# Tokens 512 to 1023 of a mixture unit as one block of 512, and the attention steps in another order

## The chip, the cores and the metric

The kernel runs on one core of one Trainium2 chip. The metric is the device time of one execution, in microseconds (us), as the median of several runs. The core has five engines with a queue each: TensorE (PE; its weight loads are listed as PEld), VectorE (DVE), ScalarE (ACT), GpSimd (POOL) and SyncE (SP, which here only issues DMAs).

## The reference, cut to what matters

```python
# 1. attention with a decaying state: B=2 batches, H=8 heads, S=768 tokens, D=48
for t in range(S):
    cur = einsum('bhd,bhe->bhde', u[None] * k[t], v[t])
    y[:, :, t] = einsum('bhd,bhde->bhe', r[t], state + cur)
    state = w[None, :, :, None] * state + einsum('bhd,bhe->bhde', k[t], v[t])
x = y.transpose(0, 2, 1, 3).reshape(1536, 384)
# 2. mixture of 4 units, all of them dense: w1[e] is 384x1024, w2[e] is 1024x384
p = probs / (probs.sum(-1) + 1e-9)
for e in range(4):
    out += p[:, e:e+1] * (relu(x @ w1[e]) @ w2[e])
# 3. one more layer pair with ELU, 384 -> 2048 -> 384
g = where(h > 0, h, exp(min(h, 0)) - 1), h = out @ w_in
return g @ w_out
```

## The kernel before, in words

Every product of the layers is computed in three matmuls, since each operand is split into a high and a low part: high times high, low times high, high times low. For weights the parts are wh and wl, for x they are xh and xl, for the hidden values hh and hl. Features lie on the partitions and tokens on the free axis.

**Units and rows.** `layers` (L877) runs over six units `u` (four of the mixture, two halves of the last pair), over blocks of tokens that start at `t0` and have `n` tokens, and over eight slices `f` of 128 hidden features. One turn of the inner loop is called a row here. A row has one group of nine matmuls into a bank `ph` (`st1`, L721, matmuls at L732), then the evacuation of ph (`evac`, L739): hh on ScalarE (L744) and hl on VectorE (L745). Two rows later follows the second product, nine matmuls into `po` (`st2`, L760, matmuls at L770); that of a block's last slice comes ahead of the row's evacuation. After a block `evac1` (L779) multiplies po by the probabilities `pb` on VectorE (L788). Two banks `ph` take turns. In the first unit, tokens 0 to 1023 are four blocks of 256 and tokens 1024 to 1535 one block of 512; in all later units every block has 512.

**Weights.** `load` and `load_next` (L541) fetch slices of 128x768 from SP's queue. `split` (L573) makes wh on ScalarE (L580) and wl on VectorE (L581). In the first unit `work` makes one such split at the end of each row until its eight slices are done. While `paced` is set, a load waits until the third load ahead of it has landed. Three raw slices have a buffer.

**Attention.** It runs in twelve chunks of 128 tokens, six for each batch, and shares the engines with the rows of the first unit. Chunks 0 and 1 come before the first row. The steps of a chunk c are:

- scaling, `s1h` (L231): r and k, transposed (rkT), by tables of powers of w, two multiplies on VectorE;
- u times k times r, `s1u` (L248, L250, tile uk), and the keys for the state, `s1k` (L241, tile kp): on POOL, from rk;
- the sum of uk over each head, `s1d` (L256), on VectorE; then the diagonal of the scores' tile A: `s1g` (L261) on POOL, `s1e` (L267) on ScalarE;
- scores, `s2` (L298), into two banks of `pa`;
- mask, `s2p` (L305): VectorE copies the scores of earlier keys from those banks into A, whose diagonal holds the sums and whose other half holds zeros;
- output, `s3` (L356): the state's part (L368), the next chunk's scores if `more` is set, the state's new part `s3u` (L320, in a ph bank), and A times v (L377); then VectorE makes the new state S (`s3s`, L341), ScalarE copies the result (yT, L384), and for every second chunk the transposed result goes through DRAM (xd, xs; L389, L393);
- state scaling, `s3w` (L353), on ScalarE, which the next `s3s` needs;
- `s4`: xh on ScalarE and xl on VectorE or POOL of 256 tokens (L534, L535).

**Order.** The order of instructions on each engine is that of the program. `fast` (L923) builds a list `steps`; `before` hands each row some of them: after the row's ph group and ahead of its evacuation (early) or behind the evacuation (late). Four banks serve the attention in turn: scores take the first two, outputs the last two (`at.own`, `bank`).

## Time and profile before

| what | value |
|---|---|
| median of 3 runs | 648.69 us (648.41 to 648.79) |
| the profiled execution | 648.31 us, its span 646.5 us |
| PE busy | 638.5 us, 99% of the span |
| PEld, DVE, ACT, POOL busy | 83%, 50%, 35%, 33% |
| granted TensorE clock, mean of the span | 0.998 |
| matmuls of 512 columns at L732, high times high | 384, 389 ns each |
| the same with 256 columns | 96, 290 ns each |

Times in the profile count from the span's first instruction. The duration of one matmul overlaps that of the next, so the pace is read from a whole group of nine and not from one matmul. An idle time is shown in square brackets ahead of the row that ended it, with what released it. The first row of the first unit begins at 16.0 us, the block of tokens 1024 to 1535 at 117.6 us.

### The profile page before, as it was taken

To read this page: it belongs to the slowest core of one execution; us is meant where nothing else is said; L and a number is where in the kernel's file an instruction comes from. 1 tells how busy PE (TensorE), PEld (TensorE's weight loads), DVE (VectorE), ACT (ScalarE), POOL (GpSimd) and SP (SyncE) were. 2 spreads that over 40 slices of the span, in tenths; PEclk is the share of its full clock that TensorE was granted. 3 is DMA by queue.
4 is the path that set the end of the run, shared out by engine and by line. 5 is a ranking of instruction groups with operands and counts; after the bars stand their busy time and mean duration, and the time that the engine had idled before them with its cause. 6 is when DMAs were issued, how large, how long until landed. Compare 5 with 4: busy or idle time off the path is not lost.

```text
span 646.5 us, 9506 instructions
## 1 busy us (share of the span) xinstructions
PE 638.5 (99%) x3843; PEld 536.9 (83%) x3845; DVE 324.8 (50%) x461; ACT 226.3 (35%) x414; POOL 210.6 (33%) x179
## 2 busy tenths in 40 slices
PE   8999999999999999999999999999999999999997
PEld 6799999888888888888888888888888888888885
DVE  7776654445545455554545456566667653112122
ACT  7732333332211131211132112123646464544441
POOL 7854672100031212130312132342754434333331
PEclk9999999999999999999999999999999999999999
DMA  8884563334131143411216231318441342001011
GB/s 243 272 289 119 153 176 114 112 99 147 49 98 30 68 154 115 167 54 50 97 58 242 99 115 50 97 34 314 190 148 37 110 146 98 1 0 50 1 50 54
DMA packets 27593, 72.72 MB, mean 112 GB/s; under 512 B 3266, under 2 KB 8436, under 8 KB 27540
## 3 DMA queue, kind: packets, MB, share of 16 engines
q1 hardware_dynamic: 22640, 59.41, 28.4%
q10 hardware_dynamic: 4900, 12.61, 5.1%
q8 instruction: 32, 0.52, 0.3%
q14 instruction: 21, 0.17, 0.1%
HBM read 55.08 MB, written 16.93 MB: 111 GB/s over the span
## 4 chain that ended last, share of the span: by engine, by line
PE 92%; DMA 5%; DVE 1%; POOL 1%; issue 1%; SPq 0%; ACT 0%; DVEq 0%
PE ph L732 44%; PE po L770 44%; DMA raw<-in_ws_dram 3%; DMA pb<-pd 1%; DMA rk<-in_rkv_dram 1%; PE po L914 1%; PE pa L298 1%; PE pa L377 1%; PE pa L368 1%; PE po L377 0%; PE ph L320 0%; SPq L543 0%; POOL uk L250 0%; POOL uk L248 0%; DVE hl L745 0%
## 5 line engine op out<-in xcount | busy, mean ns | idle before, releaser
L732 PE MATMUL ph<-xh,wh 128*128 128x512 f32 (+1 forms) x480 | 174.5, 369 | 0.4 <-DVE hl L745 0.3
L770 PE MATMUL po<-hh,wh 128*128 128x512 f32 (+1 forms) x471 | 173.9, 369 | 0.0
L732 PE MATMUL ph<-xh,wl 128*128 128x512 f32 (+1 forms) x480 | 173.8, 368 | 0.0
L770 PE MATMUL po<-hl,wh 128*128 128x512 f32 (+1 forms) x471 | 173.0, 367 | 0.0
L770 PE MATMUL po<-hh,wl 128*128 128x512 f32 (+1 forms) x471 | 173.0, 367 | 0.0
L744 ACT ACTIVATE hh<-ph 128x512 fp32r<-128x512 f32 (+1 forms) x112 | 60.0, 536 | 260.6 <-PE ph L732 260.4
L745 DVE SCALAR_TENSOR_TENSOR hl<-ph,hh 128x512 fp32r<-128x512 f32 (+1 forms) x112 | 68.4, 612 | 158.1 <-ACT hh L744 157.8
L732 PE MATMUL ph<-xl,wh 128*128 128x512 f32 (+1 forms) x480 | 124.7, 368 | 0.0
L732 PEld LDWEIGHTS ph<-xh,wh 128*128 128x128 f32 x480 | 90.4, 188 | 16.2 <-DVE hl L745 0.5
L732 PEld LDWEIGHTS ph<-xh,wl 128*128 128x128 f32 x480 | 90.5, 188 | 14.9
L770 PEld LDWEIGHTS po<-hh,wh 128*128 128x128 f32 x471 | 88.7, 188 | 16.3 <-issue 1.5
L757 POOL TENSOR_TENSOR hl<-g,hh 128x512 fp32r<-128x512 f32 x48 | 63.1, 1314 | 117.6 <-ACT hh L756 109.5
L770 PEld LDWEIGHTS po<-hl,wh 128*128 128x128 f32 x471 | 88.7, 188 | 14.7
L770 PEld LDWEIGHTS po<-hh,wl 128*128 128x128 f32 x471 | 88.7, 188 | 14.7
L732 PEld LDWEIGHTS ph<-xl,wh 128*128 128x128 f32 x480 | 85.9, 188 | 15.4 <-DVE xl L535 0.4
L643 POOL TENSOR_TENSOR nl<-a,wide 128x768 fp32r<-128x768 f32 x16 | 29.8, 1865 | 173.9 <-issue 106.1
L754 DVE SCALAR_TENSOR_TENSOR g<-m,ph 128x512 f32<-128x512 f32 x48 | 32.9, 686 | 104.6 <-ACT m L752 99.1
L792 POOL TENSOR_TENSOR acc<-acc,t 128x512 f32<-128x512 f32 x27 | 34.2, 1294 | 72.5 <-DVE t L791 72.5
L756 ACT CAST hh<-g 128x512 fp32r<-128x512 f32 x48 | 29.9, 622 | 43.0 <-DVE g L754 43.0
L751 ACT ACTIVATE m<-ph 128x512 f32<-128x512 f32 x48 | 28.7, 598 | 43.4 <-PE ph L732 36.7
L581 DVE TENSOR_TENSOR wl<-raw,wh 128x768 fp32r<-128x768 f32 x32 | 32.0, 1013 | 5.4 <-ACT wh L580 4.9
L752 ACT ACTIVATE m<-m 128x512 f32<-128x512 f32 x48 | 30.3, 632 | 1.5
(129 smaller groups left out, 487.2 us busy)
## 6 DMA issues: line engine op xcount, KB each, us to landing
raw<-in_ws_dram SPq DMA_DIRECT2D x32, 384.0 KB, 4.0
wide<-in_ws_dram SPq DMA_DIRECT2D x16, 768.0 KB, 5.1
w<-nh ACTq DMA_DIRECT2D x16, 384.0 KB, 2.4
w<-nl ACTq DMA_DIRECT2D x16, 384.0 KB, 5.7
wh<-w SPq DMA_DIRECT2D x16, 384.0 KB, 5.7
wl<-w SPq DMA_DIRECT2D x16, 384.0 KB, 6.6
rk<-in_rkv_dram SPq DMA_DIRECT2D x12, 384.0 KB, 5.8
rkT<-in_rkT_dram SPq DMA_DIRECT2D x10, 448.0 KB, 5.3
```

The source lines that it names most:

```text
L581: self.weng.tensor_tensor(out=lo, in0=t, in1=hi.bitcast(F32), op=ALU.subtract)
L643: nc.gpsimd.tensor_tensor(out=lo, in0=af, in1=cf, op=ALU.add)
L732: nc.tensor.matmul(ph[:, 0:n], a[:, kk, c0:c0 + P], b[:, kk], start=q == 0, stop=q == 3 * KD - 1)
L744: nc.scalar.activation(hh[:, 0:n], ph[:, 0:n], AF.Relu)
L745: nc.vector.scalar_tensor_tensor(out=hl[:, 0:n], in0=ph[:, 0:n], scalar=0.0, in1=hh[:, 0:n].bitcast(F32), op0=ALU.max, op1=ALU.subtract)
L751: nc.scalar.activation(m, ph, AF.Relu, scale=-1.0)
L752: nc.scalar.activation(m, m, AF.Exp, scale=-1.0)
L754: nc.vector.scalar_tensor_tensor(out=gg, in0=m, scalar=-1.0, in1=ph, op0=ALU.add, op1=ALU.max)
L756: nc.scalar.copy(hh, gg)
L757: nc.gpsimd.tensor_tensor(out=hl, in0=gg, in1=hh.bitcast(F32), op=ALU.subtract)
L770: nc.tensor.matmul(po, a[:, ff, i * P:(i + 1) * P], b[:, 0:n], start=f == 0 and q == 0 and not i * n % TB, stop=f == NF - 1 and q == 2 and ...
L792: nc.gpsimd.tensor_tensor(out=a, in0=a, in1=t[:, 0:n], op=ALU.add)
```

## The change

Tokens 512 to 1023 of the first unit become one block of 512, so the first unit has two blocks of 256 and two of 512. As this block needs x of all its tokens at its first row, the attention of chunks 0 to 7 now has to be over by the end of the second block; a table `plan` names for each block of the first unit (0, 1, 2), slice and place (E early, L late) what is done there. In it:

- the mask of a chunk stands behind the output of the chunk before it, and for chunks 3 and 4 behind rows of its own; the sum and the diagonal stand one row or more ahead of the mask. The second half of the diagonal is made on ScalarE for all chunks (`s1d`, `s1e`);
- chunk 4's scores are issued inside the output of chunk 3;
- for chunks 9 to 11, which run beside the block of 512, one result goes to a ph bank, and the state's new part comes behind A times v (`late`);
- the loads of chunks 3 and 4 stand earlier in SP's queue, between the raw slices; only the first unit's eight slices are loaded until `rest`, in the third block; pb is loaded in two pieces; after chunks 3 and 5 the next loads go ahead of the results' stores (`mid`);
- xl of s4 is made on VectorE, except after chunks 5 and 9;
- hh and hl have buffers of 512 tokens from the start; two tables of the start move to tiles that are written only later.

```diff
-NS = (3, 1, 1, 1, 1, 1, 1, 1)
...
+        self.prb = g.xp.tile([P, 2, NP, P], F32, tag="acc0", name="prb")
...
-        self.Tr = self.c.tile([P, NP, P], F32, name="Tr")
+        self.Tr = self.g.xp.tile([P, NP, P], F32, tag="acc1", name="Tr")
...
     def s1d(self, ci):
         self.a0[ci] = a0 = self.p2.tile([P, H], F32, tag="a0", name="a0")
         self.g.nc.vector.tensor_reduce(out=a0, in_=self.st[ci]["uk"], axis=AX.X, op=ALU.add)
-        for j in range(1 if ci < 4 else 2):
-            self.s1g(ci, j)
+        self.s1g(ci, 0)
...
-    def s3(self, ci, more=False):
+    def s3(self, ci, more=False, late=False, mid=None):
         g, nc = self.g, self.g.nc
         st = self.st.pop(ci)
         A, v, c = self.A[ci % 2], self.v[ci], ci % NCB
-        py = [self.bank()[:, 0:2 * P].rearrange("q (s t) -> q s t", s=2) for j in range(2)]
+        py = [b()[:, 0:2 * P].rearrange("q (s t) -> q s t", s=2) for b in (self.bank, g.new_ph if late else self.bank)]
+        self.nbank += late
...
-        pu = self.s3u(ci, g.new_ph() if ci > 2 else g.pop.tile([P, TB], F32, tag="po1", name="po1")) if c < NCB - 1 else None
+        last = c == NCB - 1
+        pu = None
+        if not late and not last:
+            pu = self.s3u(ci, g.new_ph() if ci > 2 else g.pop.tile([P, TB], F32, tag="po1", name="po1"))
...
+        if late:
+            pu = g.new_ph()
+            pu = None if last else self.s3u(ci, pu)
         self.s3s(ci, pu)
+        if mid:
+            mid()
...
-        self.g.put_x((ci - 1) // 4, (ci - 1) % 4 * P, 2 * P, self.xs, self.g.nc.vector if ci == 3 else self.g.nc.gpsimd)
+        self.g.put_x((ci - 1) // 4, (ci - 1) % 4 * P, 2 * P, self.xs, self.g.nc.gpsimd if ci in (5, 9) else self.g.nc.vector)
...
-        if self.nraw < len(self.slices):
+        if self.nraw < (len(self.slices) if self.more else 8):
...
-        self.load_next()
+        if self.auto:
+            self.load_next()
...
-    def load_pb(self, e):
-        self.pb = self.cp.tile([P, N], F32, tag="pb", name="pb")
-        self.queue.dma_start(out=self.pb, in_=self.pd[e:e + 1, :].broadcast_to([P, N]))
+    def load_pb(self, e, a=0, b=N):
+        if not a:
+            self.pb = self.cp.tile([P, N], F32, tag="pb", name="pb")
+        self.queue.dma_start(out=self.pb[:, a:b], in_=self.pd[e:e + 1, a:b].broadcast_to([P, b - a]))
...
-        hh = self.hp.tile([P, self.hw], F32R, tag="hh", name="hh")
-        hl = self.hp.tile([P, self.hw], F32R, tag="hl", name="hl")
+        hp = self.hps[self.nh % len(self.hps)]
+        self.nh += 1
+        hh = hp.tile([P, TB], F32R, tag="hh", name="hh")
+        hl = hp.tile([P, TB], F32R, tag="hl", name="hl")
...
-            m = N if u else N - TB
-            for t0, n in [(t, TB if u else tb0) for t in range(0, m, TB if u else tb0)] + [(t, TB) for t in range(m, N, TB)]:
+            m = 0 if u else 2 * tb0
+            for t0, n in [(t, tb0) for t in range(0, m, tb0)] + [(t, TB) for t in range(m, N, TB)]:
...
-            self.paced = True
+            self.paced, self.more, self.auto = True, False, False
...
             at.s1a(0)
+            at.load_T(3)
...
             pu = at.s3u(0)
+            at.load_rk(3)
+            self.load_next()
+            at.load_v(3)
...
-            load(3)
-            at.load_rk(3)
...
             at.s3f(1)
+            at.load_T(4)
+            self.load_next()
+            at.load_v(4)
...
+            at.load_rk(4)
...
-            self.paced = False
-            load(4)
-            at.load_rk(4)
...
+            self.load_next()
+            self.paced, self.auto = False, True
+            def scale(c):
+                at.s1h(c, 0)
+                at.s1h(c, 1)
+            def loads(c):
+                load(c)
+                if c < NCH:
+                    at.load_rk(c)
+            def diag(c):
+                at.s1d(c)
+                at.s1e(c)
                 at.s3w()
...
+            def keys(c):
+                at.s1k(c)
                 if c + 1 < NCH:
                     at.s1u(c + 1)
...
+            def k2(c):
+                at.s2(2)
+                at.s1e(2)
+                at.s3w()
+                at.s2p(2)
+                at.s1u(3)
+            def y2(c):
+                at.s3(2)
+                loads(5)
+                self.probs_out(lambda: self.pop.tile([P, TB], F32, tag="po0", name="po0"))
+                diag(3)
+                keys(3)
+                scale(4)
+            def out(c):
+                more, first = c + 1 < NCH, c in (3, 5)
+                at.s3(c, more, c > 8, (lambda: loads(c + 3)) if first else None)
+                if c > 3 and more:
                     at.s2p(c + 1)
...
+                    keys(c + 1)
+                if not first:
+                    loads(c + 3)
+            def rest(c):
+                self.more = True
+                for _ in range(self.NRAW):
+                    self.load_next()
+            pb = lambda c: self.load_pb(0, *((0, TB), (TB, N))[c])
+            E, L = True, False
+            plan = {
+                (0, 0, L): [(lambda c: self.probs2(dp), 0), (k2, 2), (scale, 3)],
+                (0, 1, L): [(y2, 2)], (0, 2, L): [(at.s2, 3), (at.s2p, 3)], (0, 3, L): [(out, 3)],
+                (0, 4, L): [(diag, 4), (at.s2p, 4), (keys, 4)], (0, 5, E): [(scale, 5)], (0, 5, L): [(pb, 0)],
+                (0, 6, E): [(diag, 5)], (0, 6, L): [(out, 4)],
+                (0, 7, E): [(scale, 6)], (0, 7, L): [(at.s4, 3), (diag, 6)], (1, 0, L): [(out, 5)],
+                (1, 1, E): [(scale, 7)], (1, 1, L): [(diag, 7)], (1, 2, L): [(out, 6)],
+                (1, 3, E): [(scale, 8)], (1, 3, L): [(at.s4, 5), (diag, 8)], (1, 4, L): [(out, 7)],
+                (1, 5, E): [(scale, 9)], (1, 5, L): [(diag, 9)], (1, 6, L): [(out, 8), (pb, 1)],
+                (1, 7, L): [(at.s4, 7)],
+                (2, 0, E): [(scale, 10)], (2, 0, L): [(diag, 10)], (2, 1, L): [(out, 9), (rest, 0)],
+                (2, 2, E): [(scale, 11)], (2, 2, L): [(diag, 11)], (2, 3, L): [(out, 10)],
+                (2, 4, L): [(at.s4, 9)], (2, 5, L): [(out, 11)],
+                (2, 7, L): [(at.s4, 11)]}
...
-                if u == 0 and steps:
-                    return lambda early: [run(*steps.pop()) for _ in range(
-                        t0 == 0 and f == NF - 1 if early else NS[f] if t0 == 0 else 1 + (steps[-1][0] == at.s4)) if steps]
+                if u == 0 and t0 < N - TB:
+                    return lambda early: [g(c) for g, c in plan.pop((t0 // 256, f, early), ())]
```

## Rows read from the trace of the kernel before

**Rows 1.** The page's chain that ended last: share of the span by engine.

```profile
PE 92%; DMA 5%; DVE 1%; POOL 1%; issue 1%; SPq 0%; ACT 0%; DVEq 0%
```

**Rows 2.** The chain in order of time: start us, us, what.

```profile
51.41 1.08 PE po L770 x9
...
125.95 2.04 PE po L770 x9
```

**Rows 3.** Timeline of PE and PEld: start, us, engine, line, [idle before].

```profile
27.93 0.54 PEld L320 LDWEIGHTS ph<-v,kp 128*64 128x64 f32 x16 [0.17 <-POOL kp L241]
...
29.65 0.54 PE L377 MATMUL pa<-A,v 128*48 128x128 f32 x6 [1.06 <-DVE A L305]
...
43.01 0.42 PEld L732 LDWEIGHTS ph<-xl,wh 128*128 128x128 f32 x3 [0.22 <-DVE xl L535]
...
50.07 0.39 PE L732 MATMUL ph<-xh,wh 128*128 128x256 f32 x1 [0.28 <-DVE hl L745]
```

**Rows 4.** Three stretches: PE, PEld, DVE, ACT, POOL busy, clock, DMA share, GB/s.

```profile
24.60:28.86 4.26, 3.99 (x70) 3.39 (x60) 1.93 (x4) 2.06 (x7) 4.18 (x5) 1.00 1.03 330
28.86:43.20 14.34, 13.53 (x136) 12.48 (x137) 12.72 (x18) 7.82 (x20) 9.09 (x7) 1.00 0.83 249
...
50.00:105.00 55.00, 54.79 (x771) 51.52 (x773) 31.80 (x62) 17.01 (x49) 33.03 (x30) 1.00 0.47 133
```

**Rows 5.** Timeline of PE: first matmuls of three ph groups.

```profile
32.07 0.39 PE L732 MATMUL ph<-xh,wh 128*128 128x256 f32 x1
...
36.49 0.28 PE L732 MATMUL ph<-xh,wh 128*128 128x256 f32 x1
...
39.87 0.28 PE L732 MATMUL ph<-xh,wh 128*128 128x256 f32 x1
```

**Rows 6.** The chain in order of time: one chunk's output.

```profile
81.48 0.25 PE pa L368
...
82.07 0.87 PE pa L298 x22
...
84.42 1.26 PE po L770 x9
```

**Rows 7.** Timeline of POOL: u times k of chunk 3.

```profile
23.22 1.73 POOL L248 TENSOR_TENSOR uk<-rk,ub 128x384 f32<-128x384 f32 x1 [2.33 <-DMA rk<-in_rkv_dram]
```

**Rows 8.** Timeline of DVE in the first and second block.

```profile
24.34 0.34 DVE L341 TENSOR_TENSOR S<-po,wS 112x192 f32<-112x192 f32 x1
...
26.89 0.56 DVE L256 TENSOR_REDUCE a<-uk 128x8 f32<-128x384 f32 x1 [0.57 <-POOL uk L250]
28.86 1.35 DVE L305 COPY_PREDICATED A<-mask,pa 128x512 f32<-128x512 uint8 x2 [1.42 <-POOL A L261]
...
30.42 1.27 DVE L581 TENSOR_TENSOR wl<-raw,wh 128x768 fp32r<-128x768 f32 x1 [0.20 <-ACT wh L580]
...
33.93 0.42 DVE L745 SCALAR_TENSOR_TENSOR hl<-ph,hh 128x256 fp32r<-128x256 f32 x1 [0.55 <-ACT hh L744]
34.27 0.68 DVE L231 TENSOR_TENSOR rkT<-rkT,T 112x512 f32<-112x512 f32 x1
...
35.47 0.54 DVE L256 TENSOR_REDUCE a<-uk 128x8 f32<-128x384 f32 x1
...
48.60 1.09 DVE L788 TENSOR_TENSOR acc<-po,pb 128x256 f32<-128x256 f32 x3 [3.31 <-DMA pb<-pd]
```

**Rows 9.** Timeline of ACT in the first block.

```profile
27.48 1.28 ACT L267 ACTIVATE A<-ident,a 128x128 f32<-128x128 f32 x4 [2.20 <-DVE a L256]
28.67 0.99 ACT L353 ACTIVATE wS<-S,T 112x48 f32<-112x48 f32 x4
29.57 0.82 ACT L580 CAST wh<-raw 128x768 fp32r<-128x768 f32 x1
...
33.51 0.38 ACT L744 ACTIVATE hh<-ph 128x256 fp32r<-128x256 f32 x1 [1.39 <-PE ph L732]
```

**Rows 10.** Tile wl up to 50 us: count, ns min/median/max, first and last start.

```profile
L581 DVE TENSOR_TENSOR wl<-raw,wh x8: 941/1064/1787, 14.0 to 38.3; 128x768 fp32r<-128x768 f32 x8
```

## What was expected of the change

> **What bounds the kernel now.** I read the chain that ended last first [rows 1]: 92% of it is TensorE, so a change pays only if it takes time from TensorE's own queue, and costs as soon as that queue waits. Next the same chain in order of time [rows 2]: nine matmuls on 256 tokens take 1.08 us, nine on 512 tokens 2.04 us, so 512 tokens cost 2.16 us in halves and 2.04 us in one piece. Per matmul that is 0.12 and 0.227 us: the halves stream half the columns but do not run in half the time. Then TensorE's own rows with idle time ahead of them [rows 3]: 1.06 us at 29.65 for the masked scores (A, L305), 0.22 us at 43.01 for xl, 0.28 us at 50.07 for an hl (L745). That is 1.56 us, so there is little waiting to win. Last, VectorE by stretch [rows 4]: from 28.86 to 43.20 it is busy for 12.72 of 14.34 us, later for 31.80 of 55 us. It works through its queue in order, so 89% means next to no room in the first block of rows.
>
> **1. The block of 512.** In the first unit, tokens 512 to 1023 had 2 x 8 rows of 256 and get 8 rows of 512. Each row has one group into ph and one into po: 16 groups of 2.04 us in place of 32 of 1.08 us, 16 x (2.16 - 2.04) = -1.92 us [rows 2], all of it on TensorE's queue. The evacuations of these rows get fewer and longer; VectorE is at 58% there [rows 4], which hides them. With that cover gone a row's hl would hold up the next ph but one.
> By the Trainium skill, "TensorE: Matmul & The Clock Gate", section Back-to-back issue gap, the isolated gap is N/2.4 + 2.5 ns, 109 ns for 256 columns and 216 ns for 512. By it the halves would lose only some 0.37 us over these groups (an estimate from that page). The 120 and 227 ns of the chain differ from both, and the sum goes by the chain.
>
> **2. One break fewer.** The scores of chunk 4 stood alone in the first block: from the start of one ph group at 36.49 to the next at 39.87 are 3.38 us, of which 2.16 are the two groups, so the lone scores cost 1.22 us [rows 5]. Now they stand inside chunk 3's output, where scores take 0.87 us [rows 6]: -0.35 us. Those of chunks 2 and 3 stay alone.
>
> **3. Old waits that go.** The 1.06 us came from rk of chunk 3: POOL waited 2.33 us for it [rows 7], then came u times k, its sum on VectorE at 26.89 and the diagonal, and the mask began only at 28.86 [rows 8]. The 0.28 us came from pb: VectorE stood 3.31 us for it [rows 8]; now a third of it is loaded first, and the rest is needed only at the end of the block of 512. The 0.22 us is counted anew in step 4 (d). Sum: -1.56 us. So far -1.92 - 0.35 - 1.56 = -3.83 us.
>
> **4. New waits in the first block.** The attention of chunks 3 to 6 comes earlier, and its steps now stand on VectorE and ScalarE ahead of the evacuations of the next row. I add up start-to-start times along these queues.
> (a) Output of chunk 3, row 3. It now begins with chunk 4's scores, which go into the banks that the mask of chunk 3 (L305, row 2) reads. That mask stands on VectorE behind row 2's hl; hl needs hh; and hh stands on ScalarE behind row 1's diagonal, state scaling and slice split. The chain: S, started at 24.34, leaves VectorE free at 24.68 [rows 8]. POOL is free at 23.22 - 2.33 = 20.89, and u times k took 3.67 us, from 23.22 to the sum at 26.89 [rows 7, 8], so the sum can begin at 24.7. Diagonal +0.59, state scaling +1.19, wh +0.90, wl +0.85 [rows 8, 9], wl's own 0.94 [rows 10], hl 0.34, mask 1.35 [rows 8]: 30.9. TensorE gets there at about 27.95 [rows 3]. Wait: 2.9 us. For wl I take the shortest of eight, which errs towards the new kernel; with the longest, 1.79, it is 3.8. If rk of chunk 3 lands as late as before, the sum stays at 26.89 and the wait is 5.1. Lower end 2.7.
> (b) Output of chunk 4, row 6. Chunk 5's scores need that chunk scaled (L231), which stands on VectorE behind wl of row 4, that behind wh, and that behind the state scaling and diagonal of chunk 4. From the start T of row 4's ph group: hh at T+1.44 (32.07 to 33.51), hl +0.42, sum +0.34, diagonal +0.59, state scaling +1.19, wh +0.90, wl +0.85, its own 0.94, two multiplies 1.20: T+7.87 [rows 5, 8, 9, 10]. TensorE gets there after five groups of 1.08 and 0.59 of the state's part, at T+5.99 [rows 2, 6]. Wait: 1.9 us, 2.7 with the long wl, and 1.0 if wl is out of the chain.
> (c) From the end U of that scaling: hl of row 5 0.34, wl 0.94, sum to diagonal 0.59, diagonal 1.19, hh to hl 0.42, hl of row 6 done 0.42 later, U+3.9. TensorE wants this row's bank for row 7 at U+3.61 (2.35 from scores to the next group and 1.26 for that [rows 6]). Wait: 0.3 us, between 0 and 0.5.
> (d) The second block's first row needs xl of tokens 256 to 511. VectorE: that hl begins at U+3.48; then S +0.34, 0.34, mask 1.35, scaling of chunk 6 1.20, hl 0.34, xl 0.94 (wl's shape): U+8.0. TensorE: U+3.9, two groups 2.16, and the six matmuls that don't need xl 0.72: U+6.8. Wait: 1.2 us, between the 0.2 of before and 1.6.
> What is queued behind a waiting matmul is the whole rest of TensorE's work, and it has no idle time later to give this back. Sum: 2.9 + 1.9 + 0.3 + 1.2 = +6.3 us.
> A second reading has the same sign: VectorE must put two scalings, two sums and a mask more into this block (2 x 1.20 + 2 x 0.5 + 1.35 = 4.75 us), while the stretch grows by one chunk's output, about 3 us, and was 89% full.
>
> **5. What costs nothing.** In the second block a chunk has two rows, 4 x 1.08 + 2.94 + 0.18 = 7.4 us [rows 2, 6]. VectorE needs 1.2 + 0.56 + 1.35 + 0.34 + 0.7 of them, ScalarE 1.2 + 0.9 and evacuations, so each mask is ready a row ahead; without that cover each chunk would wait like (a). The moved loads: SP's queue is in order, and rkT and rk of chunks 3 and 4 now pass slices 2 to 4. No row shows how much room slice 2 has; late, it holds up wh, and (a) grows by as much (0 to 1 us, within C's end). The later units' slices are put off to the third block, over two rows of 4.08 us ahead of their use. One diagonal of each chunk goes from POOL to ScalarE. In the third block ph serves the output too; TensorE comes to it after 2.35 us of scores and outputs, long enough for the row's evacuation (1.44 - 1.08 + 0.42 + 0.42 us for a row of 256).
>
> **The sum.** -3.83 + 6.3 = +2.5 us. The profiled execution took 648.31 us, 646.5 of them the span and 1.8 around it; the median of the runs is 648.69, 0.38 above, and I carry the step over: 651.2 us. With (a) to (d) at their ends the forecast runs from 649.9 to 652.9 (the 5.1 of (a) is C).
>
> **Rivals.**
> A. The new waits stay near the old ones, 0.4 us in all, because hh and hl get ahead of the diagonals, so that the mask of chunk 3 ends near 28. 648.69 - 3.83 + 0.4 = 645.3 us. For it: VectorE is idle for 2.3 of 4.26 us between 24.60 and 28.86 [rows 4]. Against it: ScalarE's diagonal, state scaling and wh at 27.48, 28.67 and 29.57 run in the order of the code [rows 9].
> B. Only (a) falls; behind it VectorE has caught up, and (b) to (d) are hidden: 648.69 - 3.83 + 2.9 = 647.8 us. Against it: (b) counts from TensorE's own row, so a delay ahead of it changes nothing.
> C. rk of chunk 3 lands no earlier, since the DMA queues are full (share 1.03 [rows 4]) and passing one slice gains nothing: (a) is 5.1, 651.2 + 2.2 = 653.4 us. It costs from a landing after 20.9 on.
> D. The groups of 512 save only what the page's gap leaves: as a mechanism of this kernel, a bank that comes free 0.1 us late at each of the 16 groups. 651.2 + 1.55 = 652.7 us. Against it: the steady 2.04 us [rows 2].
>
> **How the numbers follow.** Forecast 0.45, A 0.25, B 0.18, C 0.10, D 0.02. About 0.2% (1.3 us) is what a measurement can tell from no change. Faster, under 647.4, is A: 0.25. The same is B: 0.18. Slower is the forecast, C and D: 0.57. The likeliest time is 651.2 us. For 8 in 10 the range takes in A's centre and C's: 645.0 to 653.6 us.
>
> **What would show it.** Right: at L732, 48 matmuls of 256 columns for each product in place of 96, and groups of 2.04 us in the third block; TensorE idle for about 3 us ahead of scores (pa, L298) near 28, released by VectorE's A; for about 2 us ahead of scores near 41, released by rkT; for about 1 us for xl near 48; no wait in the second block. Wrong: no idle row over 1 us there (A); the first alone (B); the first at 5 us with POOL waiting for rk (C); longer groups in the third block (D).

## The result, and the profile after

The changed kernel takes 656.62 us (median of four runs, 655.06 to 657.65) against 648.74 us for the kernel before: 1.0119 times the time, 95% interval 1.0096 to 1.0141. The forecast was 651.2 us, range 645.0 to 653.6. It is slower, as forecast, but by 7.9 us where 2.5 were forecast.

The execution that was profiled took 655.06 us, 653.2 of them the span; that is 6.75 us over the profiled execution of before. The steps below are made against this one.

From the page of after, the chain that ended last, by engine:

```profile
PE 93%; DMA 3%; DVE 1%; ACT 1%; issue 1%; SPq 0%; DVEq 0%; ACTq 0%
```

TensorE still makes up the chain, as in [rows 1]; so the loss must lie in its queue. Its rows with idle time ahead of them (start us, busy us, engine, line, tiles, count, in brackets the idle time and what ended it) answer to [rows 3]. L297 writes the scores (L298 before), L742 is the first layer (L732 before).

```profile
31.49 0.43 PE L297 MATMUL pa<-rkT 48*64 48x128 f32 x2 [3.49 <-DVE A L304]
32.09 1.76 PE L297 MATMUL pa<-rkT 48*64 48x128 f32 x30 [0.17 <-DVE A L304]
46.01 1.98 PE L297 MATMUL pa<-rkT 48*64 48x128 f32 x32 [2.51 <-DVE rkT L231]
53.75 0.39 PE L742 MATMUL ph<-xh,wh 128*128 128x256 f32 x1 [0.18 <-ACT xh L542]
...
54.74 0.41 PEld L742 LDWEIGHTS ph<-xl,wh 128*128 128x128 f32 x3 [0.22 <-DVE xl L543]
```

The two long waits are where steps 4 (a) and (b) of the prediction put them and are ended by what it named: 3.66 us ahead of chunk 4's scores, ended by the mask of chunk 3 (A, L304), and 2.51 us ahead of chunk 5's, ended by that chunk's scaling (rkT, L231). The busy time of these rows has grown as well: 30 matmuls of chunk 4's scores take 1.76 us and the 32 of chunk 5's 1.98 us, where a timeline row of 32 took 1.10 us before (at 17.94; the 0.87 of [rows 6] is the chain's time). The stretches of one microsecond show why (busy time of PE, PEld, DVE, ACT and POOL with counts, then the granted clock of TensorE as a share of 2.4 GHz, DMA share, GB/s):

```profile
32.00:33.00 1.00, 0.91 (x22) 0.91 (x26) 1.00 (x3) 0.00 (x0) 0.00 (x0) 0.68 0.90 337
33.00:34.00 1.00, 1.00 (x20) 0.67 (x16) 0.21 (x1) 0.00 (x0) 0.00 (x0) 0.50 0.39 80
34.00:35.00 1.00, 1.00 (x21) 1.00 (x21) 0.08 (x1) 0.00 (x0) 0.00 (x0) 0.50 0.69 218
35.00:36.00 1.00, 1.00 (x15) 0.99 (x11) 0.28 (x1) 0.23 (x1) 0.00 (x0) 0.61 1.10 404
...
46.00:47.00 1.00, 0.99 (x20) 0.99 (x24) 1.00 (x2) 0.00 (x0) 0.00 (x0) 0.51 0.79 293
47.00:48.00 1.00, 1.00 (x22) 0.67 (x16) 0.61 (x2) 0.35 (x2) 0.24 (x1) 0.50 1.10 274
48.00:49.00 1.00, 1.00 (x19) 1.00 (x21) 0.00 (x0) 1.00 (x5) 1.00 (x2) 0.50 0.88 276
49.00:50.00 1.00, 1.00 (x17) 0.89 (x13) 0.77 (x3) 0.38 (x2) 0.92 (x2) 0.78 0.18 71
```

After each of the two waits TensorE was granted its lower level, 1.2 GHz, and worked at it for 3.4 us. What a stretch costs can be added up from the clock column: 0.32 + 0.50 + 0.50 + 0.39 = 1.71 us of TensorE's time, and 0.49 + 0.50 + 0.50 + 0.22 = 1.71 us for the second. In [rows 4] the clock stands at 1.00 throughout, and no step of the prediction has it.

Last, the chain in order of time (start us, us, what). The group of 512 tokens in the third block is the forecast 2.04 us, as in [rows 2]. The first-layer group at 83.26 has 0.3 us more, and ahead of it the chain stands on ScalarE's xh of these tokens (82.48 to 83.21).

```profile
83.26 2.35 PE ph L742 x9
...
95.09 2.04 PE po L782 x9
```

So the theory to be tested: the change moves the time by the sum of the prediction, with waits (a) and (b) a little longer, **and** by what the lower clock takes after each of them. (Where the expectations speak of a theory Q, it is this one.) Its rivals: the waits are only a sign of something else (taking them away gives nothing back); the slow scores have another cause than the wait ahead of them, such as operands that are read while other engines write; the clock falls for a reason of its own (rival C of the expectations); the block of 512 itself loses time (their rival B). The letters of the expectations aren't those of the prediction.

### The profile page after: what moved, and what is told of

It is laid out like the page before. It is cut to its first block, busy times and chain, and to the rows that moved or that the text cites. A ratio compares the mean times of both kernels' runs of the same rounds, so it can differ in the third digit from the quotient of the medians.

```text
span 653.2 us, 9220 instructions
## 1 busy us (share of the span) xinstructions
PE 639.8 (98%) x3699; PEld 532.0 (81%) x3701; DVE 327.9 (50%) x452; ACT 234.3 (36%) x438; POOL 197.6 (30%) x169
## 4 chain that ended last, share of the span: by engine, by line
PE 93%; DMA 3%; DVE 1%; ACT 1%; issue 1%; SPq 0%; DVEq 0%; ACTq 0%
PE ph L742 44%; PE po L782 44%; DMA raw<-in_ws_dram 3%; PE pa L297 1%; PE po L927 1%; PE pa L380 1%; PE ph L319 1%; DVE rkT L231 1%; PE pa L368 1%; PE po L380 0%; SPq L551 0%; ACT A L266 0%; DVE A L304 0%; ACT wS L352 0%; ACT wh L588 0%
## 5 line engine op out<-in xcount | busy, mean ns | idle before, releaser
L742 PE MATMUL ph<-xh,wh 128*128 128x512 f32 (+1 forms) x456 | 171.5, 379 | 0.5 <-ACT xh L542 0.3
L742 PE MATMUL ph<-xh,wl 128*128 128x512 f32 (+1 forms) x456 | 170.9, 378 | 0.0
L782 PE MATMUL po<-hh,wh 128*128 128x512 f32 (+1 forms) x447 | 169.7, 380 | 0.0
L782 PE MATMUL po<-hh,wl 128*128 128x512 f32 (+1 forms) x447 | 168.8, 378 | 0.0
L782 PE MATMUL po<-hl,wh 128*128 128x512 f32 (+1 forms) x447 | 168.8, 378 | 0.0
L742 PE MATMUL ph<-xl,wh 128*128 128x512 f32 (+1 forms) x456 | 123.1, 378 | 0.0
L742 PEld LDWEIGHTS ph<-xh,wh 128*128 128x128 f32 x456 | 85.7, 188 | 17.1 <-ACT xh L542 1.0
L742 PEld LDWEIGHTS ph<-xh,wl 128*128 128x128 f32 x456 | 85.8, 188 | 15.8
L782 PEld LDWEIGHTS po<-hh,wh 128*128 128x128 f32 x447 | 84.0, 188 | 17.1 <-issue 1.5
L782 PEld LDWEIGHTS po<-hl,wh 128*128 128x128 f32 x447 | 84.0, 188 | 15.6
L782 PEld LDWEIGHTS po<-hh,wl 128*128 128x128 f32 x447 | 84.0, 188 | 15.6
L742 PEld LDWEIGHTS ph<-xl,wh 128*128 128x128 f32 x456 | 83.4, 188 | 16.2 <-DVE xl L543 0.2
L652 POOL TENSOR_TENSOR nl<-a,wide 128x768 fp32r<-128x768 f32 x16 | 29.8, 1864 | 188.0 <-DVE a L651 147.2
```

Source lines behind the costliest of these rows:

```text
L652: nc.gpsimd.tensor_tensor(out=lo, in0=af, in1=cf, op=ALU.add)
L742: nc.tensor.matmul(ph[:, 0:n], a[:, kk, c0:c0 + P], b[:, kk], start=q == 0, stop=q == 3 * KD - 1)
L782: nc.tensor.matmul(po, a[:, ff, i * P:(i + 1) * P], b[:, 0:n], start=f == 0 and q == 0 and not i * n % TB, stop=f == NF - 1 and q == 2 and ...
```

## The experiments

**1. The mask of chunk 3 one row earlier.** Nothing else is changed.

```diff
                 scale(4)
+                at.s2(3)
+                at.s2p(3)
...
-                (0, 1, L): [(y2, 2)], (0, 2, L): [(at.s2, 3), (at.s2p, 3)], (0, 3, L): [(out, 3)],
+                (0, 1, L): [(y2, 2)], (0, 3, L): [(out, 3)],
```

> Chunk 3's scores and mask stand one row earlier, right behind chunk 3's diagonal, ahead of row 1's slice split and of row 2's evacuation on VectorE. Theory Q (queue order: the mask stands behind wl and hl, and the long idle time also halves TensorE's clock for 3.4 us): the wait ahead of chunk 4's scores falls from 3.66 us to some 1.2, an 0.5 us wait for the ph bank may come up, one break (0.2 to 0.3 us) goes, and if the shorter idle time keeps the clock, 1.7 us more are won: 652.5 to 654.5 us, the second wait near 46 unchanged. Rival B (the loss lies in the block of 512 and its shared ph banks): within 1 us of 656.6.

Measured: 652.23 us, 1.0057 times the time before [1.0037, 1.0077], 4.4 us less than the changed kernel. TensorE's rows with idle time:

```profile
24.64 1.10 PE L297 MATMUL pa<-rkT 48*64 48x128 f32 x32 [1.15 <-issue]
...
42.88 1.99 PE L297 MATMUL pa<-rkT 48*64 48x128 f32 x32 [2.51 <-DVE rkT L231]
```

The wait ahead of chunk 4's scores is gone; 1.15 us ahead of chunk 3's and 0.65 us ahead of the state's new part (at 31.61) take its place, and no lower clock follows either. The trace names no releaser for the first; VectorE's second multiply for chunk 3's scaling, 1.50 us from 23.04, ends 0.1 us ahead of these scores. The second wait stays at 2.51 us and so do its slow scores, 1.99 us. So the slow scores belong to the wait ahead of them. The profiled runs add up: 3.66 and 1.7 us gone, 1.15 and 0.65 new, and 0.5 more in the start-up (0.85 us for xl at 18.13, where the first profile of the changed kernel has 0.38), 3.1 us in all; the spans show 653.2 - 650.2 = 3.0.

**2. The scaling of chunk 5 one row earlier**, alone.

```diff
-                (0, 4, L): [(diag, 4), (at.s2p, 4), (keys, 4)], (0, 5, E): [(scale, 5)], (0, 5, L): [(pb, 0)],
+                (0, 4, E): [(scale, 5)], (0, 4, L): [(diag, 4), (at.s2p, 4), (keys, 4)], (0, 5, L): [(pb, 0)],
```

> The scaling of chunk 5 stands one row earlier, ahead of row 4's evacuation, where VectorE was idle; nothing else is changed. Theory Q: the wait of 2.5 to 2.7 us ahead of chunk 5's scores goes, and with it the second stretch at half clock (1.7 us): 656.6 - 4.3 = 652.3 us, the first wait (3.66 us) and its half-clock stretch unchanged. Rival C (the clock falls for a reason of its own, not for idle time): the wait goes but a second half-clock stretch near 46 stays: 654.1 us. Rival B: within 1 us of 656.6.

Measured: 653.96 us, 1.0078 [1.0058, 1.0098]. The second wait is gone; only 0.45 us at 45.39 and 1.02 us at 49.18 (the first layer, for an hl) are left there. That is what was expected, but the time came out 1.7 us too long. The stretches of four microseconds say where (columns as above):

```profile
28.00:32.00 4.00, 0.50 (x6) 0.29 (x2) 3.13 (x4) 2.12 (x5) 3.36 (x3) 0.72 0.97 257
32.00:36.00 4.00, 4.00 (x59) 3.46 (x59) 1.68 (x4) 0.00 (x0) 0.00 (x0) 0.50 0.82 263
36.00:40.00 4.00, 4.00 (x36) 3.73 (x33) 1.97 (x3) 1.86 (x4) 0.00 (x0) 0.93 1.01 296
```

The first wait is as long as it was (3.50 us, the scores start at 31.61), but the lower level lasts twice as long and begins while TensorE still waits. A stretch of one microsecond, without a matmul:

```profile
30.00:31.00 1.00, 0.00 (x0) 0.00 (x0) 1.00 (x3) 0.12 (x1) 1.00 (x1) 0.50 1.08 240
```

The clock column adds up to 4 x (0.28 + 0.50 + 0.07) = 3.4 us, but the part that lies in the wait costs nothing. From 31.61 on it is 0.2 us up to 32.00, 2.0 up to 36.00 and 0.3 behind: 2.5 us, 0.8 more than in the first profile of the changed kernel. Against that profile 2.51 and 1.7 us are gone, and 0.8, 0.45, 1.02 and 0.1 (xl, 0.34 us at 53.09) are new, 1.8 us less in all; the spans show 653.2 - 651.7 = 1.5. So what the expectation misses went to the longer stretch and to new waits. After the same wait the lower level can last 3.4 or 6.8 us.

**3. Both moves together** (the two diffs above).

> Both moves together. Theory Q: both waits and, if the rest of the first stays under 1.5 us, both half-clock stretches go: 648.0 to 650.0 us, level with the kernel before or a little under it. If the second wait only moves elsewhere because VectorE is full in the first block: 651 to 653 us. Rival B: within 1 us of 656.6.

Measured: 649.56 us over ten runs against 648.95 us for the kernel before, 1.001 [1.0001, 1.002]. 7.1 us of the 7.9 are back with two moves in the order of the work. The longest waits left:

```profile
24.62 1.10 PE L297 MATMUL pa<-rkT 48*64 48x128 f32 x32 [1.16 <-issue]
...
45.44 0.39 PE L742 MATMUL ph<-xh,wh 128*128 128x256 f32 x1 [1.01 <-DVE hl L757]
```

After the first of them, from 24 to 28 us, the granted clock stays at 1.00, and the scores take 1.10 us.

**4. The waits filled with work.** All orders are those of the changed kernel, the waits stay; but ahead of the scores of chunks 4 and 5 TensorE gets 26 and 18 matmuls that add zeros to an unused half of a bank. They compute nothing; they only keep TensorE running while it waits.

```diff
+        for _ in range({3: 26, 4: 18}.get(ci, 0)):
+            nc.tensor.matmul(
+                pf[:, 2 * P:4 * P], self.zero[:, 0:P], self.zero[:, 0:2 * P], start=False, stop=False)
         if more:
             self.s2(ci + 1)
```

> The changed kernel as it is, with 26 matmuls of zeros ahead of chunk 4's scores and 18 ahead of chunk 5's, into unused columns of an output bank: TensorE works through most of both waits without a result. Theory Q: the two waits last as long as before, but the granted clock stays at 1.0 through both, so that the 2 x 1.7 us go: 653.2 us (656.6 - 3.4). Rival C: the half-clock stretches stay: 656.6 us. If the zeros overrun the waits: up to 1 us worse than either.

Measured: 653.21 us, 1.0062 [1.0043, 1.008]: 3.4 us less than the changed kernel, as forecast, though the scores still wait for what they waited for.

```profile
32.42 0.43 PE L297 MATMUL pa<-rkT 48*64 48x128 f32 x2 [0.57 <-DVE A L304]
45.36 1.10 PE L297 MATMUL pa<-rkT 48*64 48x128 f32 x32 [0.44 <-DVE rkT L231]
...
32.00:36.00 4.00, 3.40 (x68) 2.81 (x69) 2.50 (x5) 0.70 (x3) 0.26 (x1) 1.00 0.65 186
```

The scores are still released by A and by rkT, the clock stays at 1.00, and chunk 5's scores take 1.10 us in place of 1.98. This separates the two halves of the theory: the waits cost their length, and the lower clock after them comes on top, so it doesn't fall for a reason of its own. From the first-layer group of row 3 to that of row 4, around the first wait, it takes 9.62 us (27.08 to 36.70) where the first profile of the changed kernel has 11.18 (26.17 to 37.35); from row 6 to row 7, around the second, 8.04 (41.02 to 49.06) for 9.59 (41.67 to 51.26). That is 1.56 and 1.55 us less. By the Trainium skill, "TensorE: Matmul & The Clock Gate", section HAM oscillation — how this bites in real kernels, the price of throttled time is its length times the missing share of the clock; the rows agree to some 0.15 us, with 1.71 us for a stretch of 3.4 that TensorE works through. That the medians differ by 3.4 to the tenth is in part luck: the median of the changed kernel holds more of the lower clock than its first profile (run 5), and run 4's profile starts row 3 0.9 us later, ahead of both waits.

**5. The changed kernel once more**, to see how its own time varies.

> The changed kernel once more, for its half-clock stretches. The profiled run has two of 3.41 us, and was 1.6 us faster than the median. Theory Q: runs near 656.6 us have three such lengths, as one wait can cost two of them (the run with chunk 5's scaling moved had 6.83 us at one wait): a profile near 656.6 us shows 10.2 us at half clock before 60 us, one near 655 us shows 6.8.

Measured: 657.03 us (656.16 to 657.47), 1.0123 [1.0106, 1.014]. Its profiled execution has the waits of the first one (3.49 and 2.52 us), one of 0.68 us for the mask at 22.15, and this clock after the second wait:

```profile
44.00:48.00 4.00, 1.48 (x39) 1.24 (x31) 4.00 (x6) 0.78 (x2) 1.59 (x1) 0.83 0.96 283
48.00:52.00 4.00, 4.00 (x50) 3.31 (x46) 2.39 (x7) 2.27 (x7) 3.01 (x3) 0.50 0.45 135
52.00:56.00 4.00, 3.87 (x27) 3.66 (x25) 1.62 (x4) 1.12 (x3) 0.00 (x0) 0.81 0.00 0
```

4 x (0.17 + 0.50 + 0.19) = 3.4 us: the long stretch again, this time at the second wait. It begins just ahead of the wait's end at 46.86, and costs 3.3 us behind it. Together with the 1.7 of the first that is 5.0 us. At half the clock TensorE is for 2 x (3.4 + 1.7) = 10.2 us, as expected of a time near 656.6 us. The span is 2.4 us over that of the first profile, 1.6 of it from here and 0.7 from the mask. This fits the other executions of the changed kernel, which lie 1.1 to 2.6 us above the one that was profiled first and have a mean granted clock of 0.990 to 0.993 where that one has 0.995; only two of the eight have a profile.

**6 to 8. More moved at once.** The next try moved five steps, and with one of them a weight split: scaling of chunk 3 ahead of the mask of chunk 2, the mask of chunk 3 to the start of row 2, scaling of chunk 5 earlier, the diagonal of chunk 5 later, copies of x earlier, and the weight split of row 1 to row 3.

```diff
-                        self.work(0.9 if not u else 1.2)
+                        self.work({1: 0, 3: 1.8}.get(f, 0.9) if not u and not t0 else 0.9 if not u else 1.2)
...
                 at.s3w()
+                scale(3)
                 at.s2p(2)
...
+                (0, 1, L): [(y2, 2)], (0, 2, E): [(at.s2, 3), (at.s2p, 3)], (0, 3, L): [(out, 3)],
+                (0, 4, E): [(scale, 5)], (0, 4, L): [(diag, 4), (at.s2p, 4), (keys, 4)], (0, 5, L): [(pb, 0)],
+                (0, 6, L): [(diag, 5), (out, 4)],
+                (0, 7, E): [(at.s4, 3), (scale, 6)], (0, 7, L): [(diag, 6)], (1, 0, L): [(out, 5)],
...
+                (1, 7, E): [(at.s4, 7)],
```

> The block of 512 and the attention plan stay; five steps stand elsewhere in the queues: chunk 5's scaling a row earlier; chunk 3's scaling ahead of chunk 2's mask; chunk 3's scores and mask ahead of row 2's evacuation, with row 1's slice split put behind it; chunk 5's diagonal behind row 6's evacuation; xh and xl of chunks 2, 3 and 6, 7 a row's evacuation earlier. Theory Q: against the run with both moves (649.6 us) the waits of 1.16, 0.65 and 1.01 us and parts of those for xh and xl go, no half-clock stretch comes back: 645.5 to 647.5 us, under the kernel before. If VectorE is simply full in the first block, whatever the order, the waits move to other places: 649 to 650 us.

Measured: 651.89 us, 1.0058 [1.0038, 1.0078]. A miss, by 5 us. The wait ahead of chunk 4's scores is gone, but a new one came. ScalarE's row and TensorE's:

```profile
43.96 0.83 ACT L588 CAST wh<-raw 128x768 fp32r<-128x768 f32 x1 [3.44 <-DMA raw<-in_ws_dram]
...
46.18 0.39 PE L742 MATMUL ph<-xh,wh 128*128 128x256 f32 x1 [1.72 <-DVE hl L757]
```

A split also issues the next weight slice's load. Moved two rows back, that load fell behind chunk 3's write and read of x through DRAM on SP's queue (xd issued at 32.87, xs at 39.52 us) and was issued at 40.00 us; in run 3 it stood ahead of them (two loads from 31.18 on). The slice came 3.44 us late for ScalarE; hh and hl stand behind its cast in ScalarE's and VectorE's queues, and so TensorE stood.

The same with blocks of 256 for tokens 512 to 1023 was meant to price the block of 512 (`m = 0 if u else N - TB`).

> The same five moves, but tokens 512 to 1023 again as two blocks of 256: only the block of 512 is undone. By the step of the sum, 16 x 0.12: 1.9 us above the run with the five moves. Rival B or the smaller gain of 0.37 us: level with it, or under it.

Measured: 657.43 us, 1.0125 [1.0108, 1.0142], 5.5 us over run 6. That is no price of a block. The late slice cost more in this run:

```profile
45.13 0.83 ACT L588 CAST wh<-raw 128x768 fp32r<-128x768 f32 x1 [5.38 <-DMA raw<-in_ws_dram]
...
47.34 0.58 PE L742 MATMUL ph<-xh,wh 128*128 128x256 f32 x1 [3.67 <-DVE hl L757]
...
48.00:52.00 4.00, 4.00 (x21) 4.00 (x21) 3.03 (x5) 2.59 (x8) 2.91 (x3) 0.50 0.55 144
```

That is 1.95 us more of wait, and 6.8 us at the lower level that run 6's profile doesn't have; they begin in the wait (near 45.6, TensorE starts at 47.34) and cost 2.6 us behind it. Besides, the attention of chunks 9 to 11 keeps its row numbers and so stands in the eight rows of tokens 512 to 767 alone, where waits of 1.60 and 0.83 us come up (L319, at 89.25 and 96.61). This run settles nothing about the block.

The third of these has run 6's order with weight slice 2 loaded ahead of rkT of chunk 3.

```diff
             at.s1a(0)
+            self.load_next()
             at.load_T(3)
...
             at.load_rk(3)
-            self.load_next()
             at.load_v(3)
```

> The five moves, and raw slice 2 loaded ahead of rkT and rk of chunk 3, as in the kernel before. ScalarE's wait for that slice in the first row (0.79 us in the changed kernel) goes; theory Q with VectorE's queue as what binds: 0.3 to 0.7 us under the run with the five moves. If rk of chunk 3 then lands after 21 us and u times k becomes late, as in the kernel before: 0.5 to 2 us above it.

Measured: 651.75 us, 1.0046 [1.0031, 1.006], level with run 6. It opened another wait at once:

```profile
23.48 0.64 PE L380 MATMUL pa<-A,v 128*48 128x128 f32 x8 [1.93 <-DVE A L304]
...
24.00:28.00 4.00, 4.00 (x46) 3.49 (x46) 3.70 (x7) 2.50 (x9) 3.19 (x4) 0.61 0.84 241
```

Now rkT of chunk 3 came late (VectorE waited 1.53 us for it at 21.50), and with the scaling of chunk 3 ahead of it the mask of chunk 2 came late too. The wait of 1.93 us was again followed by a stretch at the lower level, 4 x 0.39 = 1.6 us in these four microseconds. Run 6's late slice is there as well: ScalarE waits 3.64 us for it (45.78) and TensorE 1.93 us for hl (47.99), again with 3.4 us at the lower level behind it. What slice 2's place is worth by itself stays open.

**9. The block of 512 by itself.** Run 3's order, with tokens 512 to 1023 as two blocks of 256; the block's attention is spread over the sixteen rows so that each piece comes at about the time it had, and weight splits come every second row.

```diff
-            m = 0 if u else 2 * tb0
+            m = 0 if u else N - TB
...
-                        self.work(0.9 if not u else 1.2)
+                        self.work((0.9 if t0 < TB else 0.9 * (f % 2)) if not u and t0 < N - TB else 0.9 if not u else 1.2)
...
+                (2, 0, E): [(scale, 10)], (2, 1, L): [(diag, 10)], (2, 3, L): [(out, 9), (rest, 0)],
+                (2, 4, E): [(scale, 11)], (2, 5, L): [(diag, 11)], (2, 7, L): [(out, 10)],
+                (3, 1, L): [(at.s4, 9)], (3, 3, L): [(out, 11)],
+                (3, 7, L): [(at.s4, 11)]}
```

> The changed kernel with both waits taken out as in the run that gave 649.56 us (mask of chunk 3 and scaling of chunk 5 earlier), but with tokens 512 to 1023 of the first unit as two blocks of 256 again; the attention work of the block is spread over the sixteen rows so that each piece comes at about the same time as before, and the weight splits come every second row. It measures the block of 512 alone: by the groups of the first layer, 16 x (2.16 - 2.04) = 1.9 us more, so about 651.5 us (651.0 to 652.5). If the block of 512 saves nothing (the rival), 649.6 us.

Measured: 652.59 us, 1.0063 [1.0049, 1.0077], 3.0 us over run 3 (2.9 by the spans). 0.95 us of it are a wait of its own, of the state's part of chunk 9's output for a ph bank that hl frees:

```profile
85.95 0.32 PE L368 MATMUL ph<-rkT,S 48*64 48x128 f32 x1 [0.95 <-DVE hl L757]
```

2.9 - 0.95 = about 2.0 us remain, against 1.92 in the prediction. But the two profiles differ already where the programs are still the same: the first row of the second block starts at 48.04 us in run 3 and at 47.38 here.

```profile
48.04 0.38 PE L742 MATMUL ph<-xh,wh 128*128 128x256 f32 x1 [0.18 <-ACT xh L542]
...
47.38 0.39 PE L742 MATMUL ph<-xh,wh 128*128 128x256 f32 x1 [0.18 <-ACT xh L542]
```

From that row to the end this run takes 603.4 us and run 3 599.8: 3.6 us more, 2.6 without the wait. The groups account for 1.92 of them; what the rest is, no row here shows. So the block of 512 saves 2.0 to 2.6 us, no less than step 1 said.

**10 to 12. The waits that run 3 has left.** The mask of chunk 3 to the start of row 2 (behind row 1's weight split), the diagonal of chunk 5 behind row 6's evacuation, the copies of x for chunks 2 to 3 and 6 to 7 earlier, and run 2's move:

```diff
-                (0, 1, L): [(y2, 2)], (0, 2, L): [(at.s2, 3), (at.s2p, 3)], (0, 3, L): [(out, 3)],
-                (0, 4, L): [(diag, 4), (at.s2p, 4), (keys, 4)], (0, 5, E): [(scale, 5)], (0, 5, L): [(pb, 0)],
-                (0, 6, E): [(diag, 5)], (0, 6, L): [(out, 4)],
-                (0, 7, E): [(scale, 6)], (0, 7, L): [(at.s4, 3), (diag, 6)], (1, 0, L): [(out, 5)],
+                (0, 1, L): [(y2, 2)], (0, 2, E): [(at.s2, 3), (at.s2p, 3)], (0, 3, L): [(out, 3)],
+                (0, 4, E): [(scale, 5)], (0, 4, L): [(diag, 4), (at.s2p, 4), (keys, 4)], (0, 5, L): [(pb, 0)],
+                (0, 6, L): [(diag, 5), (out, 4)],
+                (0, 7, E): [(at.s4, 3), (scale, 6)], (0, 7, L): [(diag, 6)], (1, 0, L): [(out, 5)],
...
-                (1, 7, L): [(at.s4, 7)],
+                (1, 7, E): [(at.s4, 7)],
```

> The changed kernel with the mask of chunk 3 issued at the start of row 2 (ahead of that row's evacuation, but behind the second scaling multiply of chunk 4), the scaling of chunk 5 one row earlier, the diagonal of chunk 5 behind row 6's evacuation instead of ahead of it, and the copies of x for chunks 2 to 3 and 6 to 7 at the start of row 7. Against the version with the first two moves alone in another form (649.56 us) it should lose the 1.16 us wait ahead of the scores of chunk 3 down to about 0.3, the 1.01 us wait of the first layer behind row 6's hl at 45.4 us, and the 0.18 and 0.33 us waits for x: 649.6 - 0.9 - 1.0 - 0.5 = about 647.3 us, 646.5 to 648.5, with no stretch at half clock. That would be under or level with the kernel before. If the waits only move (the rival: each queue has too much ahead of it whatever the order), it stays at 649 to 651 us.

Measured: 651.59 us, 1.0044 [1.003, 1.0057], a miss: the wait ahead of chunk 4's scores is back, 3.17 us where the changed kernel has 3.49. VectorE's rows and TensorE's:

```profile
28.77 1.71 DVE L589 TENSOR_TENSOR wl<-raw,wh 128x768 fp32r<-128x768 f32 x1 [0.92 <-ACT wh L588]
30.40 1.32 DVE L304 COPY_PREDICATED A<-mask,pa 128x512 f32<-128x512 uint8 x2
...
31.17 0.43 PE L297 MATMUL pa<-rkT 48*64 48x128 f32 x2 [3.17 <-DVE A L304]
```

The start of row 2 is still behind row 1's split. VectorE waits 0.92 us for wh, makes wl for 1.71 us, and only then the mask. So that split was moved behind row 2, one row and not two, so that its load keeps its place on SP's queue ahead of chunk 3's output:

```diff
+                        self.work({1: 0, 2: 1.8}.get(f, 0.9) if not u and not t0 else 0.9 if not u else 1.2)
```

> The version of 651.59 us (mask of chunk 3 at the start of row 2, scaling of chunk 5 and copies of x earlier, diagonal of chunk 5 later), with the split of a weight slice that stood behind row 1 moved behind row 2, so that VectorE goes from the scaling of chunk 4 straight to the mask of chunk 3, without the 0.92 us wait for wh and the 1.71 us wl between them. If that wl was what put the mask late, the mask ends 2.63 us sooner (29.1 instead of 31.7 us), the wait of 3.35 us ahead of the scores of chunk 4 shrinks to about 0.6, and its stretch at half clock (1.7 us) goes: 651.6 - 2.7 - 1.7 = about 647.2 us, 646.5 to 648.5. If the two splits behind row 2 now come too late for the layer that reads them, the wait moves to row 3 or 4 and the time stays at 649 to 651 us.

Measured: 648.37 us (11 runs), 0.9991 [0.9982, 1.0] against 649.03 us. The long wait and its stretch are gone; the row that answers to the one above reads:

```profile
29.36 0.43 PE L297 MATMUL pa<-rkT 48*64 48x128 f32 x2 [0.54 <-DVE A L304]
```

This shows what made the mask of chunk 3 late: the wl ahead of it on VectorE, with the wait for wh. The last one keeps run 3's place for the mask (ahead of that wl) and adds only the later diagonal and the earlier copies of x.

> The version of 649.56 us (mask of chunk 3 ahead of the row's wl, scaling of chunk 5 one row earlier) with the diagonal of chunk 5 behind row 6's evacuation and the copies of x for chunks 2 to 3 and 6 to 7 at the start of row 7. The 1.01 us wait of the first layer at 45.4 us behind ScalarE's diagonal copies and hl of row 6 should go, as it did in the version of 651.59 us, and the waits for x (0.18 and 0.33 us) may shrink: 649.6 - 1.0 - 0.2 = about 648.4 us (647.8 to 649.0), level with the kernel before. If the first layer's wait has another cause than the diagonal, 649.5 us.

Measured: 648.02 us (12 runs, 647.41 to 649.45) against 649.03 us, 0.9987 [0.9979, 0.9996]. The first layer's 1.01 us wait for hl is gone, as expected: the diagonal ahead of hh on ScalarE was its cause (the copies of x stand behind row 6's evacuation in both runs). This is the shortest time of all; it is under the kernel before, but by less than 0.2%, so it counts as level. Its profiled span, 646.0 us, can be set against the prediction's own terms: -3.83 from steps 1 to 3; then the waits that are left, 1.15 (24.47), 0.66 (31.43), 0.43 (41.50) and 0.53 us (47.67); 0.3 for xh in the third block; and 0.5 in the start-up (0.86 us at 17.96 for xl, where the profiles of before and of the changed kernel have 0.39 and 0.38 us). The sum is -0.3 us; the spans show 646.0 - 646.5 = -0.5.

## Why the prediction was right or wrong

**Steps 1 to 3, the gains: right.** Products of 256 columns fell to 48 of each kind, groups of 2.04 us stand in the third block, and run 9 measures 2.0 to 2.6 us for the block against 1.92, of which the excess isn't explained. The lone scores of step 2 are gone: the groups of rows 4 to 6 start 2.16 us apart (37.35, 39.51, 41.67). The old waits of 1.06 and 0.28 us are gone: rk of chunk 3 is there when POOL comes to it (u times k starts at 20.67 without a wait, in place of 23.22 [rows 7]), so rival C is out. Rivals A and B are out as both long waits came. Rival D, that the groups of 512 save nothing, is out by run 9.

**Step 4 (a), 2.9 us forecast, 3.66 measured.** TensorE got there at 31.49 - 3.49 = 28.00 us, where the prediction said 27.95. The mask was later than forecast. VectorE's rows of after beside [rows 8, 10]:

```profile
22.37 1.50 DVE L231 TENSOR_TENSOR rkT<-rkT,Kd 112x512 f32<-112x512 f32 x1
...
24.99 0.34 DVE L340 TENSOR_TENSOR S<-po,wS 112x192 f32<-112x192 f32 x1
...
28.76 1.70 DVE L589 TENSOR_TENSOR wl<-raw,wh 128x768 fp32r<-128x768 f32 x1 [0.92 <-ACT wh L588]
...
30.72 1.31 DVE L304 COPY_PREDICATED A<-mask,pa 128x512 f32<-128x512 uint8 x2
```

S began at 24.99 where step 4 took 24.34, because the multiply ahead of it took 1.50 us; before, the same operation took 0.68. And wl took 1.70 us: step 4 used the shortest of eight, 0.94, and said that the longest would give 3.8. Both grew while POOL ran:

```profile
21.75 1.56 POOL L250 TENSOR_TENSOR uk<-uk,rk 128x384 f32<-128x384 f32 x1
...
28.65 0.99 POOL L248 TENSOR_TENSOR uk<-rk,ub 128x384 f32<-128x384 f32 x1
```

POOL's uk ended at 23.31, and the multiply, which started at 22.37, ended at 23.87, 0.56 us behind it. POOL's next uk ended at 29.64, and wl, which started at 28.76, ended at 30.46, 0.82 us behind it. By the Trainium skill, "SBUF — State Buffer", section SBUF: two separate sides, VectorE with two inputs in SBUF and GpSimd share a port pair, and whichever comes second waits for the whole instruction of the first. The rows agree: about the length of one undisturbed operation (0.68 and 0.94) is left when POOL is done. The same bringing forward of rk that removed POOL's wait put its work beside VectorE's. In run 8, where POOL stands idle for rk until 23.10, the same multiply at 22.11 takes 0.69 us. No run was made for this alone. Together the two rows end the mask at 32.03 us, 1.1 later than the 30.9 of the prediction; TensorE starts behind the first of the mask's two copies, so that the wait grows by 0.76.

Step 5 let slice 2 add to (a) if it came late. ScalarE waited 0.79 us for it (wh at 21.14), but VectorE came to that slice's wl only at 23.79, so it added nothing.

**Step 4 (b), 1.9 us forecast, 2.51 measured.** The order of the chain was right to the last link. The chain of after passes through it in this order (start us, us, what; the short pieces between are left out):

```profile
37.51 1.09 PE ph L742 x9
...
38.69 0.39 ACT hh L756
39.11 0.42 DVE hl L757
39.53 0.47 DVE a L256
...
40.02 0.78 ACT A L266 x3
...
41.30 0.91 ACT wS L352 x4
42.21 0.73 ACT wh L588
...
43.87 1.00 DVE rkT L231
...
45.27 0.69 DVE rkT L231
...
46.01 1.98 PE pa L297 x32
```

With T = 37.51, the group's start in the chain, the prediction has TensorE there at T + 5.99 = 43.50; it was 46.01 - 2.51 = 43.50. It has the scaling done at 45.38; it was done at 45.96. The 0.6 us between are in the first of the two multiplies, which took 1.48 us beside POOL's uk (43.21 to 44.80) instead of 0.68, less 0.2 us saved on the links ahead.

**Step 4 (c) and (d), 1.5 us forecast, 0.4 measured.** No wait for row 7's bank is seen, and for xh and xl only 0.18 + 0.22 us. Probably the longer (a) and (b), and the slower work behind them, gave VectorE time to catch up: where (b) was taken away, the first of them came back: 1.02 us in run 2 and 1.01 in run 3, there with the diagonal of chunk 5 as its cause (run 12).

**The missing term.** The prediction's sum priced a wait at its length. Each of the two waits also took TensorE's clock to the lower level, 1.71 us a time in the first profile. The whole sum for that execution: -3.83 + 3.66 + 2.51 + 0.4 + 0.6 (two groups of the third block at 2.35 and 2.34 us) = +3.3, and + 3.4 for the clock = +6.8 us; measured 6.75. Without the clock the profiled execution would have come to about 651.6 us, inside the range; run 4, which takes the lower clock away and leaves the waits, gives 653.21, also inside, with the later start of its profile (0.9 us) in it. So the direction and the two mechanisms were right, and the step that failed is step 4's price of a wait. Of the 4.25 us between forecast and profile (6.75 - 2.5) the clock is 3.4; the VectorE rows taken at their undisturbed length are 1.4 (0.76 in (a), 0.61 in (b)), the third block 0.6, and (c) and (d) give 1.1 back. In the second profile the clock is 5.0.

**The range.** With (a) to (d) at the ends that step 4 names, the sum gives 2.7 + 1.0 + 0 + 0.2 = 3.9 to 3.8 + 2.7 + 0.5 + 1.6 = 8.6 us, so 648.8 to 653.5 us and not 649.9 to 652.9. That slip changes nothing here: 656.62 us lies above both, by the clock.

**Where the gain went.** The change does save 3.8 us. Its order of the first block gave them back and more. With that order mended (run 12) 0.5 us of them is left by the spans and 1.0 by the medians; most of the rest goes to waits of 0.4 to 1.2 us in the first block of rows, in which VectorE has next to no room.

## What to carry to other kernels

A new wait on the bounding TensorE is to be priced twice: by its length, and by the time at the lower clock that can follow it (here 1.7 to 3.3 us behind waits of 1.9 to 3.7 us; in the profiles nothing behind those of 1.72 and less). If such a wait can't be removed, matmuls that add nothing give the second half back. And when a step is moved in an engine's queue, everything that stands behind it moves as well: the loads it issues (run 6), what stands ahead of it in its new place (the wl of run 10), and the engine with which it will now overlap.

## What the runs showed of the hardware

The granted clock had only two values around the waits, 1.00 and 0.50. In the profiles, waits of TensorE of 1.06 us (before), 1.16 and 1.01 us (run 3) and 1.72 us (run 6) were not followed by the lower one; waits of 1.93 (twice in run 8), 2.51, 3.17 (run 10), 3.49 and 3.67 us (run 7) were. Run 6 had seven executions, and one that was not profiled took 655.77 us at a mean clock of 0.993, so its wait may not always pass without.

The lower level lasted 3.4 or 6.8 us. Where it began at the end of the wait or behind it, it lasted 3.4 us: in the first profile of the changed kernel twice, in runs 1 and 10, at both waits of run 8 and at the first of run 5. In the three places where it began while TensorE still waited it lasted 6.8 us: run 2 (from near 29.8, TensorE starts at 31.61), the second wait of run 5 (46.7, 46.86) and run 7 (45.6, 47.34). What lies in the wait costs nothing, so the price was 1.7 us behind 3.49 us of wait in the changed kernel and 2.5 us behind 3.50 in run 2, and 1.7 and 3.3 us behind 2.51 and 2.52 in the two profiles of the changed kernel. The same program therefore varies by some 1.6 us from one execution to the next, and the length of the wait alone doesn't tell which comes. Adding zeros kept the clock at 1.00 as well as real work did (run 4).

A multiply of two tiles on VectorE that took 0.68 us alone took 1.50 and 1.48 us beside POOL's uk, and ended some 0.55 us behind it.
